# A rebuilt prologue for a transformer block on one core: two key halves, dummy products, four tiles normalised on GpSimd

## The chip, the cores and the metric

The kernel runs on one core of one Trainium2 chip. The metric is the device time of one execution in microseconds. The core has a tensor engine (PE, with its weight loads shown apart as PEld), VectorE (DVE), ScalarE (ACT), GpSimd (POOL) and SyncE (SP). SP issues nearly all DMAs here. Matrix products write into eight PSUM banks, from which DVE or ACT move results to the on-chip memory (SBUF).

## The reference, cut to what matters

One transformer block with 2048 tokens, width 1024, 32 heads of 32 columns which share one key head and one value head, and a gated feed-forward layer of 3584. All inputs are bf16. A conditioning row `c` gives six modulation vectors: shift, scale and gate for attention, and the same for the feed-forward layer.

```python
mod = (_silu(c) @ w_mod).reshape(c.shape[0], 6, 1, -1)
sa, ca, ga, sb, cb, gb = (mod[:, 0], ..., mod[:, 5])
h = _layernorm(x, axis=-1) * (1 + ca) + sa
q = (h @ wq) split into 32 heads; k = h @ wk; v = h @ wv      # one K and one V for all heads
p = softmax(q k^T * 32 ** -0.5, axis=-1)
x = x + ga * ((p v) merged @ wo)
h = _layernorm(x, axis=-1) * (1 + cb) + sb
x = x + gb * ((_silu(h @ w1) * (h @ w3)) @ w2)
```

## The kernel before, in words

**The planner.** `build` describes every instruction as a node of a graph (`G.add`) with its engine, what it reads and writes, a modelled duration and a priority (a lower number goes first). `Dag.schedule` is a list scheduler: it runs the graph on modelled engines and thereby fixes the order of instructions on each engine and the PSUM bank of each product group. `Dag.emit` then writes one instruction stream per engine with semaphore waits. So the order on every engine is fixed before the run, and an engine waits in that order. Products of scores (class S), of probabilities with V (class V) and of denominators (class D) go ahead of others on PE. A look-ahead for DVE stands at lines 205 to 216, but is switched off by `LOOK = 0.0` (line 13).

**The prologue (lines 454 to 825).** Tokens come as 16 tiles of 128 in `X`, which has 8 slots (`NXS`). For each tile `ln` computes LayerNorm statistics (on DVE by L509 and L511, for the tiles in `ONACT` on ACT by L519 and L523), a factor `RS` on POOL (L530, L532) and the normalised tile on DVE (L544). `tr` transposes four tiles at a time on PE (L558) into PSUM and evicts them into `HT` on ACT (L569) or DVE (L572). The modulation is not applied to the tokens: the scale `1 + ca` is multiplied into the rows of wq, wk, wv (L719, L721, L750), and the shift becomes a bias of each projection (L693 to L713, L741). Both come from the product L677 of `silu(c)` with eight slabs of w_mod, 512 KB each. `ORDER` (line 644) is the order of the loads behind the first eight X tiles:

```python
ORDER = ("w0", "w1", "w2", "w3", "x8", "x9", "w4", "x10", "x11", "w5", "w6", "w7", "q", "x12", "x13", "x14", "x15")
```

"w" is a slab of w_mod, "x" a token tile, "q" the first 128 columns of wq; the other 896 columns and wo follow. K (L608, evicted by L612) is made for 256, 256, 512, 512 and 512 tokens, V (L619, L622) four times for 512 tokens, Q (L629, L632) for 8 groups of four heads (f = 0 to 7), for the first 512 tokens in two parts. `gate` (L782, L787) makes two further modulation vectors, L794 multiplies wo by one of them, and L809 and L817 make the other two. The Q projections of the later tokens come last.

**Attention (lines 830 to 959).** It runs over 8 blocks of 256 query tokens. In a block, for each f, eight steps of 256 keys: scores (L855, eight small products into four of six PSUM banks), two exponentials on ACT (L865, 128x1024 elements each) into one of `NU = 11` buffers `U`, and tree adds of four steps' buffers into one of four `TR` buffers on DVE (L879, L884), with a fold of the two trees (L889) for f below 7. At the end of an f come its products with V (L902), and the denominator products of the f before with a selection matrix `SEL` (L922). L929 copies the numerators into `ASB`. When a group of f's is complete, L946 takes reciprocals, L952 spreads them over partitions and L957 multiplies; `RP` sets the priority of these for a block's last group (one value each for the first, the middle and the last blocks).

**After attention (`post`).** The output projection (L996, L1000), LayerNorm again, for the first and last block transposition on PE with eviction (L558, L581 or L575), then gate and up products (L1030), tanh (L1039) and multiplications on DVE (L1037, L1042, L1047), then the down product (L1064, L1070, L1076). `BP` sets the DVE priority of the part up to the transposition, again by block. Their weights come in a ring of six buffers (`RING`), which take over memory of the prologue: the first three need all Q projections done. `post` of a block overlaps attention of the next; only the last one stands alone.

Of the kernel before, what the change touches and what calls it, by code (L numbers as in the profile page):

```python
# [12 lines left out]
LOOK = 0.0  # L13
# [15 lines left out]
class Dag:  # L29


    def __init__(self, nc):
        self.nc = nc
        self.nodes = []
        self.last_write = {}
        self.readers = {}
        self.seq = 0
        self.dma_sems = {}
        self.last_acq = {}
        self.chain = 0  # L40

# [64 lines left out]
    def schedule(self, banks):  # L106
# [41 lines left out]
        while left:  # L148
# [56 lines left out]
            if e == "dve" and LOOK and n.dur > 0.9 and n.prio > 1:  # L205
                fin = None
                for b in banks:
                    g = bank_group[b]
                    rem = [x for x in g.nodes if x.start is None and x.eng == "pe"] if g is not None else []
                    if rem:  # L210
                        f1 = t_free["pe"] + sum(x.dur for x in rem) + 0.26
                        if fin is None or f1 < fin:
                            fin = f1
                if fin is not None and t < fin < t + LOOK:
                    t_free["dve"] = fin
                    continue
            ready[e].remove(n)
# [132 lines left out]
def build(nc, x_in, wq_in, wk_in, wv_in, wo_in, w1_in, w3_in, w2_in, c_in, wmod_in, out, S, D, F):  # L350
# [34 lines left out]
    BP = (0, 0, 0)  # L385
    WP = (4, 4, 4)
    RP = (0, 0, 0)
# [6 lines left out]
    RB = sb("RB", [P, QB], F32)  # L394
    WKR = sb("WKR", [P, NC, 4, 32], BF16)
    ASB = XN[:, 2:4, :].rearrange("p a d -> p (a d)").bitcast(F32).rearrange("p (a q) -> p a q", a=4)
    DSB = WKR[:].rearrange("p c a f -> p (c a f)").bitcast(F32).rearrange("p (a q) -> p a q", a=2)
# [25 lines left out]
    NR = len(RING)  # L423
    assert NF * QB + 2 * 4096 <= NC * S and NXS == 8
# [5 lines left out]
    WQ0R = WKR[:].rearrange("p c a f -> p c (a f)")  # L430
    WQ0K = ["WKR"]
# [20 lines left out]

    cuts = {}
    G.add("pool", lambda e: e.memset(SEL[:], 0.0), writes=["SEL"], dur=0.3)
    for a, fs in enumerate(DGRP):
        edge = [32 * j // len(fs) for j in range(len(fs) + 1)]
        for j, f in enumerate(fs):
# [4 lines left out]
    G.add("pool", lambda e: e.memset(IDENT[:], 0.0), writes=["IDENT"], dur=0.2)  # L462
    G.add("pool", lambda e: e.affine_select(IDENT[:], IDENT[:], pattern=[[-1, P]], compare_op=ALU.not_equal,
                                            fill=1.0, base=0, channel_multiplier=1),
          reads=["IDENT"], writes=["IDENT"], dur=0.4)

# [5 lines left out]
    def xload(t0, n):  # L472
        r = []
        for t in range(t0, t0 + n):
            r.append(dma(lambda e, t=t: e.dma_start(X[:, t % NXS, :], x2[t * P:(t + 1) * P, :]),
                         ("x", t % NXS), writes=[("X", t % NXS)], nbytes=P * D * 2))
        return r

    WQK = [("WREG", "q")]
    xload(0, 8)  # L480

    def wmload(k, after=()):
        return dma(lambda e, k=k: e.dma_start(WM01[:, k, :], wmod_in[k * P:(k + 1) * P, 0:2 * D]), ("wm01", k),
            writes=[("UR", k)], nbytes=P * 2 * D * 2, after=after)
# [50 lines left out]
    def xnt(q):  # L535

        return XN[:, q, :] if q < 4 else UREG[:, (NU + NTR - 2) * 2048 + (q - 4) * D:][:, 0:D]

    def xnk(q):
        return [] if q < 4 else [("UR", NU + NTR - 2 + (q - 4) // 2)]  # L540

    def ln_norm(t, q, s=None, bp=0):
        s = t % NXS if s is None else s
        G.add("dve", lambda e: e.tensor_scalar(xnt(q), X[:, s, :], MV[:, t, 0:1], RS[:, t:t + 1],  # L544
                                               ALU.subtract, ALU.mult),
              reads=[("X", s), ("RS", t), ("MV", t)], writes=[("XN", q)] + xnk(q), dur=0.42, prio=2 - bp)

    def ln_transpose(nt, q0, dst, dkeys, fs, fm, engs, prio=5, cbs=None, allow=None, bp=0):
# [3 lines left out]
        for cb in range(NC // ncb) if cbs is None else cbs:  # L552
            g = grp(allow)
            for i in range(nt):
# [6 lines left out]
                G.add("pe", tr, reads=[("XN", q0 + i), "IDENT"] + xnk(q0 + i), dur=ncb * 0.065, lat=0.2,  # L561
# [41 lines left out]
    def kproj(t0, n, allow=None):  # L603
        sl = slice(t0, t0 + n)

        def kmm(e, b, c):
            for gg in range(4):
                r = e.matmul(b[32 * gg:32 * gg + 32, 0:n], WKV[:, 0, c, :], HT[:, c, sl], start=c == 0, stop=c == NC - 1,  # L608
                             tile_position=(0, 32 * gg), skip_group_check=True)
            return r  # L610
        g = mm_group(NC, kmm, lambda c: WKK + hk(c, t0, n), n_cols=n, allow=allow, mode="V")
# [533 lines left out]
```

## Time and profile before

| | us |
|---|---|
| median of 4 runs (lowest to highest) | 1167.51 (1167.43 to 1167.62) |
| the profiled execution | 1167.55 |
| its span in the profile | 1165.7 |

| engine | busy us | share of the span |
|---|---|---|
| PE | 1114.3 | 96% |
| DVE | 1012.9 | 87% |
| ACT | 1028.4 | 88% |
| POOL | 43.0 | 4% |

The profile is of one execution. Times in it count from the start of its span. "Busy" of PE comes from modelled ends of pipelined products, so that a busy PE may still wait a little between them. In groups of instructions, a row names the line, the engine, the operation, the output and the inputs, how often it ran, and what ended the idle time before it (in square brackets after "<-"). The granted clock is that of the tensor engine, 1.00 being full speed. Attention's exponentials are 975.3 us of ACT's busy time; the first starts at 35.66 us and the last ends at about 1055.5.

### The profile page before, as it was taken

Reading aid. Unit: us, or ns where it says so; the run is one execution under the profiler, and the core shown is the slowest. Engines: PE = TensorE matmul, PEld = TensorE weight load, DVE = VectorE, ACT = ScalarE, POOL = GpSimd, SP = SyncE. Lnnn points to the kernel's source line nnn. Section 1 sums busy time; section 2 is a strip of 40 time slices with the busy share of each in tenths; the row PEclk is TensorE's granted clock in tenths of the full one; section 3 lists DMA queues with packets and bytes.
Section 4 is the critical chain, followed back from the end, with each engine's and each line's share of the span. In section 5 each row is a group of like instructions: output and inputs, shape, how many; then the busy total and the mean of one; then the engine's idle time right before and its main releaser. Section 6 shows DMA issues by size and latency. Waiting matters only on the chain.

```text
span 1165.7 us, 34946 instructions
## 1 busy us (share of the span) xinstructions
PE 1114.3 (96%) x15532; PEld 755.7 (65%) x15561; DVE 1012.9 (87%) x1504; ACT 1028.4 (88%) x1174; POOL 43.0 (4%) x86
## 2 busy tenths in 40 slices
PE   4998996999989999999999999999999999999998
PEld 4554442666657675767576766767567757677887
DVE  7778988898999999899989998999989998997452
ACT  3798999999999999999999999999999999992110
POOL 5100000000010001000000001000100000000000
PEclk9798998899999999999999999999999999999999
DMA  9616007455757565966596566856596659656995
GB/s 346 220 29 199 12 1 182 128 163 166 198 145 222 155 184 134 265 173 188 143 255 193 162 186 176 241 160 181 145 255 174 190 138 255 196 158 182 297 292 152
DMA packets 383222, 211.05 MB, mean 181 GB/s; under 512 B 21600, under 2 KB 374880, under 8 KB 383072
## 3 DMA queue, kind: packets, MB, share of 16 engines
q1 hardware_dynamic: 380992, 208.69, 63.7%
q8 instruction: 122, 2.00, 0.7%
q10 hardware_dynamic: 2080, 0.13, 0.1%
q14 instruction: 28, 0.23, 0.1%
HBM read 201.46 MB, written 4.19 MB: 176 GB/s over the span
## 4 chain that ended last, share of the span: by engine, by line
PE 74%; ACT 15%; DVE 8%; issue 2%; POOL 1%; DMA 0%; SPq 0%
PE PB L1030 24%; PE PB L1064 15%; ACT UREG L865 13%; PE SP L855 11%; PE PB L902 8%; PE PB L629 4%; PE PB L996 3%; PE SP L1030 3%; DVE UREG L884 2%; PE SP L1064 2%; DVE UREG L879 1%; PE PB L922 1%; PE PB L608 1%; DVE ST L509 1%; PE SP L558 1%
## 5 line engine op out<-in xcount | busy, mean ns | idle before, releaser
L865 ACT ACTIVATE UREG<-SP 128x1024 bf16<-128x1024 f32 x1024 | 975.3, 1121 | 17.2 <-PE SP L855 15.0
L884 DVE TENSOR_TENSOR UREG<-UREG 128x2048 bf16<-128x2048 bf16 x256 | 311.4, 1216 | 11.9 <-ACT UREG L865 9.6
L855 PE MATMUL SP<-QT,KT 32*128 32x256 bf16 x4096 | 206.1, 276 | 15.7 <-ACT UREG L865 14.4
L1030 PE MATMUL PB<-QT,WREG 128*128 128x256 bf16 x1632 | 205.4, 273 | 0.8 <-DVE WKR L940 0.4
L1030 PEld LDWEIGHTS PB<-QT,WREG 128*128 128x128 bf16 x1632 | 148.1, 98 | 46.8 <-issue 31.5
L879 DVE TENSOR_TENSOR UREG<-UREG 128x2048 bf16<-128x2048 bf16 x128 | 156.0, 1219 | 13.2 <-ACT UREG L865 9.7
L855 PEld LDWEIGHTS SP<-QT,KT 32*128 32x128 bf16 x4096 | 60.9, 92 | 139.0 <-ACT UREG L865 93.8
L1030 PE MATMUL PB<-QT,HREG 128*128 128x256 bf16 x1056 | 132.9, 273 | 0.6 <-DVE WKR L940 0.4
L902 PE MATMUL PB<-UREG,V 128*32 128x256 bf16 x4032 | 130.8, 277 | 1.4 <-ACT UREG L865 1.4
L902 PEld LDWEIGHTS PB<-UREG,V 128*32 128x32 bf16 x4032 | 99.9, 98 | 26.6 <-issue 17.1
L1030 PEld LDWEIGHTS PB<-QT,HREG 128*128 128x128 bf16 x1056 | 96.1, 98 | 29.6 <-issue 19.6
L1064 PE MATMUL PB<-WREG,HREG 128*128 128x256 bf16 x840 | 104.9, 273 | 0.5 <-DVE HREG L1042 0.5
L1064 PEld LDWEIGHTS PB<-WREG,HREG 128*128 128x128 bf16 x840 | 77.8, 98 | 22.2 <-issue 12.6
L1030 PE MATMUL PB<-QT,X 128*128 128x256 bf16 x544 | 69.1, 273 | 1.1 <-DVE WREG L1037 0.7
L889 DVE TENSOR_TENSOR UREG<-UREG 128x2048 bf16<-128x2048 bf16 x56 | 68.1, 1217 | 0.4
L629 PE MATMUL PB<-HREG,WREG 128*128 128x512 bf16 (+1 forms) x301 | 63.7, 349 | 4.0 <-DVE QT L632 1.6
L1064 PE MATMUL PB<-HREG 128*128 128x256 bf16 x532 | 67.1, 273 | 0.0
L1039 ACT ACTIVATE GSB<-GSB 128x512 bf16<-128x512 bf16 x56 | 42.3, 756 | 28.1 <-DVE GSB L1037 28.1
L1039 ACT ACTIVATE WREG<-WREG 128x512 bf16<-128x512 bf16 x56 | 43.4, 776 | 20.1 <-DVE WREG L1037 20.1
L1030 PEld LDWEIGHTS PB<-QT,X 128*128 128x128 bf16 x544 | 49.8, 98 | 15.8 <-issue 10.7
L1064 PEld LDWEIGHTS PB<-HREG 128*128 128x128 bf16 x532 | 49.2, 98 | 13.7 <-issue 7.8
L929 DVE COPY XN<-PB 128x256 f32<-128x256 f32 x63 | 26.5, 420 | 36.0 <-PE PB L922 34.1
(130 smaller groups left out, 1005.1 us busy)
## 6 DMA issues: line engine op xcount, KB each, us to landing
WREG<-in_B_w_dram SPq DMA_DIRECT2D x112, 512.0 KB, 5.1
HREG<-in_B_w_dram SPq DMA_DIRECT2D x74, 512.0 KB, 5.3
WREG<-in_B_w_dram SPq DMA_DIRECT2D x33, 896.0 KB, 5.0
X<-in_B_w_dram SPq DMA_DIRECT2D x38, 512.0 KB, 5.0
HREG<-in_B_w_dram SPq DMA_DIRECT2D x21, 896.0 KB, 5.3
X<-in_B_w_dram SPq DMA_DIRECT2D x10, 896.0 KB, 5.0
X<-in_A_x_dram SPq DMA_DIRECT2D x32, 256.0 KB, 5.4
WREG<-in_w_mod_dram SPq DMA_DIRECT2D x16, 512.0 KB, 5.3
```

The source lines that it names most:

```text
L629: g = mm_group(NC, lambda e, b, c: e.matmul(b[:, 0:n], WQ[:, c, f * P:(f + 1) * P], HT[:, c, sl], start=c == 0, stop=c == NC - 1), lambda ...
L855: r = e.matmul(SP[:, b, o:o + qn], KT[32 * gg:32 * gg + 32, kts[j] * P:(kts[j] + 1) * P], QT[32 * gg:32 * gg + 32, f, q0:q0 + qn], start=T ...
L865: G.add("act", lambda e, u=u, h0=h0, n=n, b0=b0, nb=nb: e.activation(U[:, u, h0 * W:(h0 + n) * W].rearrange("p (b w) -> p b w", b=nb), SP[ ...
L879: G.add("dve", lambda e, tr=tr, u=u, fu=first_u: e.tensor_tensor(TR[:, tr, 0:4 * W], U[:, fu, 0:4 * W], U[:, u, 0:4 * W], ALU.add), reads= ...
L884: G.add("dve", lambda e, tr=tr, u=u: e.tensor_tensor(TR[:, tr, 0:4 * W], TR[:, tr, 0:4 * W], U[:, u, 0:4 * W], ALU.add), reads=[("TR", tr) ...
L889: G.add("dve", lambda e, ta=ta, tb=tb: e.tensor_tensor(TR[:, ta, 0:4 * W], TR[:, ta, 0:4 * W], TR[:, tb, 0:4 * W], ALU.add), reads=[("TR", ...
L902: r = e.matmul(PB[g.bank][32 * gg:32 * gg + 32, 0:qn], V[:, kt, :], U[:, pu, (gg * npk + j) * qn:(gg * npk + j + 1) * qn], start=w0 + n == ...
L929: G.add("dve", lambda e, g=g, f=f: e.tensor_copy(ASB[:, f % 4, 0:qn], PB[g.bank][:, 0:qn]), writes=[("ASB", f % 4), ("XN", 2 + f % 4 // 2) ...
L996: g = mm_group(NC, lambda e, b, f, t=t, h=h: e.matmul(b, QT[:, f, t * P:(t + 1) * P], WO[:, f, h * 512:(h + 1) * 512], start=f == 0, stop= ...
L1030: return e.matmul(b[:, j * qn:(j + 1) * qn], w13[:, w, c, j * P:(j + 1) * P], QT[:, c, q0:q0 + qn], start=c == 0, stop=c == NC - 1)
L1039: G.add("act", lambda e, b=b: e.activation(TB[b], GS[b], ACT.Tanh, scale=0.5), reads=[("GS", b)], writes=[("TB", b)], clear=alias("TB") if ...
L1064: G.add("pe", lambda e, g=g, j=j, fc=fc, hf=hf, first=first, w2s=w2s: e.matmul(PB[g.bank][:, j * 256:(j + 1) * 256], HHT[:, hf * NH + fc, ...
```

## The change

Seven things are done at once.

1. **Loads.** The slabs of w_mod are cut into a half with the scale ("a") and a half with the shift ("s"). All 16 X tiles, the halves and three parts of wq (128, 384 and 512 columns) are in one `ORDER`. wq is loaded into the memory of wo (`WO`) and scaled from there into `WQ`; wo itself is loaded after the last of these reads. The scaled wk and wv have a memory of their own (`WKS`).
2. **Scale before shift.** The product with w_mod is in two groups, scale first; scaling of wk and of the first part of wq needs the scale alone. The biases come in three parts (`bias`).
3. **Normalised tiles** have 16 places instead of 8 (`xnt`, in memory not yet used). Tiles 9, 11, 13 and 15 are normalised on POOL. Statistics on ACT are now those of tiles 2 and 5. Tiles 0 to 7 are evicted by ACT, 8 to 15 by DVE. The first transposition of a group of four tiles waits for all four.
4. **Key halves.** In the first block f = 0 to 3 run over the first four steps of keys one after another, then over the other four; then f = 4 to 7 as before. For these eight pieces there are no tree adds: the denominator products read `U` directly, four buffers a piece. Numerators and denominators of the second piece are added to those of the first.
5. **Dummy products.** While the modelled time is below 250 us, the planner fills gaps on PE with 128-column products of the identity matrix into a bank that is free.
6. **Look-ahead for DVE** with new rules, for the whole kernel: before an operation of over 0.9 us (modelled; in the steady blocks the tree adds and folds) DVE waits up to 0.5 us for one of top priority, or up to 0.6 us for a product group in bank 0 or 1, if neither bank is free within 0.5 us.
7. **Priorities.** `BP` and `RP` are 5 for the first block, which puts the end of its attention and its second LayerNorm ahead of the tree adds on DVE. There the spreading of reciprocals has a buffer for each f, so that all are spread and then all multiplied.

```diff
-LOOK = 0.0
+LOOK = 0.5
+LK = 0.6
+LF = 0.5
+UP = -1
...
-            if e == "dve" and LOOK and n.dur > 0.9 and n.prio > 1:
...
+            if e == "dve" and n.dur > 0.9 and n.prio > UP:
+                soon = [c for c in cands if c[1].prio <= UP and c[0] < t + LOOK]
+                if soon:
+                    t_free[e] = min(c[0] for c in soon)
+                    continue
+                fin = t + LK
+                for b in (0, 1):
+                    i = bank_idle(b)
+                    if i is not None and i <= t + LF:
+                        fin = None
+                        break
                     g = bank_group[b]
...
+                        fin = min(fin, t_free["pe"] + sum(x.dur for x in rem) + 0.26)
+                if fin is not None and t < fin < t + LK:
+                    t_free[e] = fin
                     continue
+            if e == "pe" and self.warm is not None and t < self.warm[0]:
+                gap = s - t_free[e] - 0.3 - (0.1 if mode != "F" else 0.0) - (0.1 if n.mode != "F" else 0.0)
+                fb = [x for x in free_banks() if x[0] + SEM_LAT <= t_free[e]]
+                k = int(gap / self.warm[1])
+                if k > 0 and fb and self.warm[3].start is not None and self.warm[3].vis + SEM_LAT < t_free[e]:
...
+                    w.fn = self.warm[2](b, k)
+                    w.deps = [self.warm[3]]
+                    if bank_group[b] is not None:
+                        w.deps += [x for x in bank_group[b].nodes if x.eng != "pe"]
...
-    BP = (0, 0, 0)
+    BP = (5, 0, 0)
     WP = (4, 4, 4)
-    RP = (0, 0, 0)
+    RP = (5, 0, 0)
+    RBQ = (0,)
...
+    WARM = 250.0
+    HEAD = 4
+    DIRECT = (0, 1)
...
-    def ln_norm(t, q, s=None, bp=0):
+    def ln_norm(t, q, s=None, bp=0, en="dve"):
...
-        G.add("dve", lambda e: e.tensor_scalar(xnt(q), X[:, s, :], MV[:, t, 0:1], RS[:, t:t + 1],
+        G.add(en, lambda e: e.tensor_scalar(xnt(q), X[:, s, :], MV[:, t, 0:1], RS[:, t:t + 1],
...
-    ONACT = (3, 6)
...
+    ONACT = (2, 5)
+    ONPOOL = (9, 11, 13, 15)
+    KP = 1
+    QACT = 1
+    TRP = 1
+    EV = (("act",), ("act",), ("dve",), ("dve",))
+    ORDER = ("x0", "x1", "x2", "x3", "x4", "x5", "a0", "a1", "x6", "a2", "a3", "x7", "a4", "a5", "a6", "a7", "q0",
+             "s0", "s1", "s2", "s3", "s4", "s5", "s6", "s7", "q1", "x8", "x9", "x10", "x11", "x12", "x13", "x14", "x15", "q2")
+    QCUT = (0, 1, HEAD, NC)
...
+    def qscale(k):
+        a, b = QCUT[k] * P, QCUT[k + 1] * P
...
+        for c in range(NC):
+            wr = [("WQ", f, c) for f in ((HEAD,) if k == 2 else range(1, HEAD))]
+            if k == 1 and c % 2 < QACT:
+                G.add("act", lambda e, c=c: e.activation(WQ[:, c, a:b], WO[:, c, a:b], ACT.Identity, scale=MODC[:, 1, c:c + 1]),
...
+    bias(0, (0,), kb=True)
+    G.chain = 0
+    kproj(0, 256, (2, 3, 4, 5, 6, 7))
+    qproj(0, 256, 0, (2, 3, 4, 5, 6, 7), prio=1)
+    kproj(256, 256, (2, 3, 4, 5, 6, 7))
+    kproj(512, 512, (1,))
+    wscale(1, WVK)
+    qscale(1)
+    bias(1, (0,), vb=True)
+    qproj(0, 256, 1, (0, 1))
+    vproj(0, (0, 1))
+    vproj(1, (0, 1))
...
+        def step(f, s):
+            pend, trs = pends[f], trees[f]
+            direct = q0 == 0 and f < HEAD and s // per_t in DIRECT
...
+            pend.append((u, kts))
+            if direct:
+                return
...
+            if direct:
+                ds.append((f, pend, h))
+                dprev[0] = None
...
+                            a = U[:, a[0]] if us else TR[:, a]
...
+        if q0 == 0:
+            head = []
+            for h in range(2):
+                for f in range(HEAD):
+                    head += [(f, s) for s in range(h * per_t, (h + 1) * per_t)] + [(f, (h,))]
+            sched = head + [x for x in sched if x[0] >= HEAD]
...
+    def warm(b, k):
+        def f(e):
+            for _ in range(k):
+                r = e.matmul(PB[b][:, 0:P], IDENT[:], IDENT[:], start=True, stop=True, skip_group_check=True)
+            return r
+        return f
+    G.warm = (WARM, P / 2400.0 + 0.0026, warm, ident)
```

## The prediction

> **What bounds the kernel now.** I read the busy line by stage first, then the chain of waits that ended last, then the order of time of the first 62 us. Each row of the stage view below gives a stretch, its length, the busy time of PE, PEld, DVE, ACT and POOL, the granted TensorE clock (1.00 is full) and the DMA's share and rate.
>
> ```profile
> 0.00:35.66 35.66, 19.97 (x361) 16.68 (x365) 28.79 (x71) 14.62 (x27) 16.14 (x48) 0.90 0.99 353
> 35.66:60.00 24.34, 21.73 (x394) 13.19 (x390) 16.95 (x33) 20.12 (x26) 2.20 (x6) 0.79 0.51 162
> 60.00:170.00 110.00, 102.12 (x1378) 50.02 (x1390) 94.29 (x127) 105.71 (x113) 0.00 (x0) 0.95 0.20 64
> 170.00:211.00 41.00, 29.13 (x439) 13.55 (x440) 33.66 (x57) 36.63 (x39) 2.49 (x4) 0.79 0.52 129
> 211.00:383.00 172.00, 166.03 (x2416) 112.66 (x2411) 158.38 (x223) 171.31 (x196) 3.43 (x4) 1.00 0.63 176
> 383.00:1053.00 670.00, 667.09 (x9532) 455.90 (x9543) 625.18 (x902) 666.71 (x758) 17.15 (x20) 1.00 0.68 188
> 1053.00:1165.70 112.70, 108.26 (x1032) 93.70 (x1031) 55.62 (x98) 13.26 (x21) 1.58 (x4) 1.00 0.89 230
> ```
>
> From 383 us on PE and ACT are both full (667.1 and 666.7 of 670). The chain of waits runs on ACT's exponentials from about 223 to 383 and stays on PE afterwards, one step of it being:
>
> ```profile
> 543.75 0.33 PE SP L855 x8
> 544.08 1.96 PE PB L1030 x17
> ```
>
> So two engines are matched. A second saved early reaches the end only if both gain it: ACT has 1024 exponentials to run, PE has its products. PE's loss is all early: idle 15.7 us to 35.66, then 2.6, 7.9 and 11.9 us to 211, and 6.0 us to 383. A slow clock costs more: (1 - clock) times busy is 2.0 + 4.6 + 5.1 + 6.1 us. That is 44 + 18 = 62 us in all. ACT's early loss: no exponential before 35.66, 4.2 us idle to 60, 4.3 to 170, 4.4 to 211. The lines that show why:
>
> ```profile
> 24.29 0.55 PE L677 MATMUL PB<-SCT,UREG 128*128 128x1 bf16 x16
> 35.66 9.52 ACT L865 ACTIVATE UREG<-SP 128x1024 bf16<-128x1024 f32 x10 [0.47 <-PE SP L855]
> 45.01 2.37 ACT L569 ACTIVATE HREG<-PB 128x512 bf16<-128x512 bf16 x4
> 49.33 1.89 PE L629 MATMUL PB<-HREG,WREG 128*128 128x256 bf16 x8 [0.86 <-ACT HREG L569]
> 55.22 15.69 ACT L865 ACTIVATE UREG<-SP 128x1024 bf16<-128x1024 f32 x17 [4.05 <-PE SP L855]
> 175.94 7.21 SPq L1023 DMA_DIRECT2D WREG<-in_B_w_dram  x6
> 205.81 2.63 DVE L581 TENSOR_SCALAR QT<-PB,MODC 128x256 bf16<-128x256 bf16 x8
> 211.14 1.59 PE L1030 MATMUL PB<-QT,WREG 128*128 128x256 bf16 x13
> ```
>
> The modulation product waits for its last weights until 24.3; K, Q and the first exponential follow it. From 45 to 55 ACT evicts tiles 12 to 15 and then starves. From 176, when the last Q projection lets the gate/up weights load, to 211 PE has only attention and the output projection.
>
> **What the Trainium skill says.** "TensorE: Matmul & The Clock Gate", Part 1: the array is clocked at half rate after an idle window of about 3.4 us, full rate after as much sustained activity. The trace agrees: at 49.33 eight 256-column products took 1.89 us (0.236 each) at a granted 0.63, where 17 take 1.96 (0.115) at 1.00. "GPSIMD Engine Reference", Specifications: GpSimd shares its SBUF interfaces with VectorE, contention coming with two-input or two-port instructions. The trace agrees: a one-element RS op at 202.40 took 1.13 us under a tree add, 0.22 elsewhere. Section 3.1 there gives 1.8 cycles an element for a tight loop. "DMA: Bandwidth & Descriptors" puts the ceiling at 435 GB/s; here the first 20 us reach 390 to 420.
>
> **The change, part by part.**
>
> (a) Loads. Before the scale half of the modulation is complete there now lie 8 X tiles and 8 half slabs of 256 KB, 4.2 MB, then the first Q slice, then 2.1 MB of shift halves: 6.6 MB with K and V weights. Before it was 7.3 MB, with both halves finishing at 24.3. In 2-us slices the load curve of before has moved 4.35 MB by 14 us and 6.75 by 20, and a load lands 1 to 1.5 us after its bytes (w4, 5.4 MB in order, was consumed at 17.56). So scale at 15, shift at 21. SP issues 25 loads at 0.45 us from 0.72, all by 13 us: no bound.
>
> (b) First exponential. DVE normalises six of tiles 0 to 7 by about 18.5 (six times 1.28 + 0.2 of statistics, eight times 0.54, from 4.3). ACT then evicts all 16 banks' halves, 0.52 each, the last four tiles' by 23. Shift at 21.3, products 0.3, SAB copy 0.16, bias products 0.8, copy 0.15, K and Q evictions 0.47 + 0.48 at 24, S 0.4: first exponential at about 25 instead of 35.66, 10.7 earlier. The KT of keys 512 to 1023 is needed two steps (3.7 us) later and is there at 26 to 27.
>
> (c) Key halves. The head (f 0 to 3, keys 0 to 1023) is 32 exponentials, 29 us at 0.917, so ACT needs the keys of tiles 8 to 15 only at 54. They land by 29 (9.6 MB). Their DVE work is 8 x 1.48 of statistics, 4 x 0.54, 16 evictions x 0.41: 20 us, done by about 47. So the hole from 45 to 55 goes, 4.2 us idle and 4.3 of evictions (8 x 0.54), against about 1.7 for four Q scalings on ACT (4 x 384 elements, at the evictions' rate). ACT +6.7.
>
> (d) GpSimd. Four normalisations leave DVE, 4 x 0.54 = 2.2 us in a stretch where DVE is not last: worth nothing by itself. A GpSimd one isn't in the trace. From below: POOL's 128x512 copy took 0.61, so 1.2 for 1024. By the skill's 1.8 cycles at its 1.2 GHz: an estimate of 1.5. From above: 1.5 plus one 1.2-us hold under a two-input DVE op, 2.7. I take 1.5. Queued behind on POOL are the RS ops of the next tiles; two of them late by 1.5 still end before 54. With 2.7 it is 11 us of POOL and the 7-us cover is about used up. Price if gone: 0 to 4 us.
>
> (e) Denominators of the head by PE from U directly: per f 64 small products instead of 8 or 16. By L922's 8 in 0.22 us that is 1.77 against 0.22, times 4: PE +6.2, and splitting V's groups about +1 in switches. It takes 28 tree operations of 1.22 from DVE (34 us), adds 8 x 0.41.
>
> (f) Dummy products in PE's planned gaps, until the planner's 250 us. They replace idle time, so cost nothing where plan and chip agree; they also keep the clock up. At best they return most of the 18 us of slow clock, at worst (at half rate 0.107 for 0.056 each by the clock-gate page, in gaps the chip doesn't have) they delay PE by a few us. I take 14 us returned.
>
> (g) Priorities of block 0's ending. Reciprocals, shuffles and LayerNorm go ahead of the tree adds. From the last denominator product (173.6) to the first gate/up product (211.1) passed 37 us; the pure work is about 20 (copies 0.8, two reciprocals 1.9, two shuffles and multiplies 1.7, output projection 8 between attention steps, LayerNorm 4, evictions 2.6). As the Q projections would now end near 160 and attention of block 0 near 147, the two meet, and only the 7 us of weight load remain with little to do. PE idle there 5 instead of 11.9; ACT idle 4.4 down to 1.4.
>
> (h) DVE's look-ahead holds a tree add up to 0.6 us for a finishing PE group, in every block. In a steady block DVE is busy 117.4 of 126 us, so 8.6 us are free; 56 tree adds and folds can each wait 0.15 us before it bounds. Zero to 0.1 us each is hidden; above that see rival D.
>
> Sum, PE: idle 44 to about 29 (11 in the first 25 us, 3 to 60, 4 more to the boundary, 5, 6), so -15; slow clock -14; (e) +7: -22. ACT: 10.7 + 6.7 + 2 (half of the 4.3) + 3 = -22.4. They agree by chance of the balance; PE may also gain up to 8 us over ACT, since 12 us of the previous block's down projection fill its wait at the end. For a static order made from modelled durations I take off 2: -20 against the profiled execution's 1167.55 (span 1165.7 and 1.85 around it), which is the median to 0.04. Predicted 1147.
>
> **Rivals.** A, the sum: 1147, own range 1139 to 1155. Chance 0.58.
> B, only the start survives: PE stays saturated with Q projections until about 172 and the head's 7 us eat the clock gain; -10.7 and little else, 1157 (1155 to 1163). For it: PE is 93% busy from 60 to 170. Against: the holes after 170 are then still filled. 0.17.
> C, all early loss but the first 11 us is recovered: 62 - 11 - 7 - 12 (what ACT cannot give) = 32, 1135 (1129 to 1139). For it: the boundary's 37 us. Against: weights still load after the last Q projection. 0.12.
> D, slower: the look-ahead makes DVE the bound in steady blocks. 8.6 us a block are free; at a mean wait of 0.21 us for 56 operations DVE needs 129.2, 3.2 us a block more than 126, and over seven blocks that eats the 20 and more; at 0.25 us it is 5.4 x 7 - 20 = 18 us slower, 1185. For it: DVE is the third engine near full. Against: evictions of PE's groups seldom make it wait now (0.5 us a block before L1042). 0.10.
> E, no change: gains given back at the last block's tail, within 0.2% (2.3 us, about what a measurement of this kernel can tell from no change). 0.03.
>
> **Numbers.** 1147 is the likeliest case. The range, 1133 to 1160, takes in A, most of B and half of C. Faster 0.87, same 0.03, slower 0.10.
>
> **What would show it.** First exponential near 25 us (b); no ACT idle over 2 us before 60 (c); POOL tensor_scalar of 1024 elements at 1.2 to 2.7 us (d); granted clock 0.95 or more in each stretch to 211 (f); first gate/up product near 175 (g); 126 us a block after 383 (h). A first exponential after 30, a block over 127, or PE waiting at dummy products while attention is ready would make the prediction wrong.

## The result, and the profile after

| | before | changed |
|---|---|---|
| median of all runs beside each other | 1168.75 us (58 runs) | 1166.64 us (37 runs) |
| ratio, 95% interval | | 0.9977 (0.9970 to 0.9983) |
| span of the profiled execution | 1165.7 us | 1165.7 us |

The change saves 0.23%, 2.7 us of 1168.75, where 20 were forecast and the range ended 7 us below the time before. The profiled executions happen to have equal spans (the one before lies 1.2 us below its kernel's median, the changed one 0.9 above), so their stages can be laid side by side.

The stage view of the changed kernel, in the columns of the prediction (a stretch, its length, then the busy time of PE, PEld, DVE, ACT and POOL with the number of instructions, the granted clock, the DMA share and GB/s):

```profile
0.00:25.00 25.00, 18.02 (x314) 16.68 (x315) 14.44 (x33) 13.08 (x24) 11.37 (x38) 0.87 0.98 327
25.00:60.00 35.00, 24.74 (x488) 16.04 (x486) 24.21 (x63) 22.87 (x28) 21.53 (x20) 0.79 0.36 119
60.00:170.00 110.00, 103.53 (x1617) 55.24 (x1625) 71.94 (x114) 101.11 (x107) 0.00 (x0) 0.96 0.32 102
170.00:211.00 41.00, 38.51 (x537) 19.90 (x540) 39.84 (x68) 40.30 (x44) 3.31 (x4) 1.00 0.29 72
211.00:383.00 172.00, 163.42 (x2377) 110.07 (x2378) 155.55 (x219) 170.66 (x194) 3.48 (x4) 0.97 0.69 190
383.00:1053.00 670.00, 666.51 (x9532) 456.20 (x9541) 623.32 (x903) 667.44 (x758) 17.15 (x20) 1.00 0.68 188
```

Three things are to be seen. From 383 on the busy times of each engine agree within 2 us: nothing that the change gains is lost in the steady blocks. The boundary from 170 to 211 is nearly full now (PE 38.51 of 41, of it 0.90 dummies; before 29.13). And the stretch from 25 to 60, which was to be the full one, has PE idle for 10.3 us and the clock at 0.79.

What happens there stands in the view in order of time; these rows answer to the prediction's rows of before (what an instruction waited for is in brackets):

```profile
24.71 0.40 PE L713 MATMUL PB<-SCT,UREG 128*128 128x1 bf16 x8
29.16 3.83 ACT L925 ACTIVATE UREG<-SP 128x1024 bf16<-128x1024 f32 x4 [0.69 <-PE SP L915]
43.16 3.80 POOL L573 TENSOR_SCALAR WREG<-X,MV,RS 128x1024 bf16<-128x1024 bf16 x1
43.19 1.43 DVE L573 TENSOR_SCALAR WREG<-X,MV,RS 128x1024 bf16<-128x1024 bf16 x1
47.67 3.80 POOL L573 TENSOR_SCALAR WREG<-X,MV,RS 128x1024 bf16<-128x1024 bf16 x1
51.00 0.40 PE L915 MATMUL SP<-QT,KT 32*128 32x256 bf16 x8 [0.66 <-ACT UREG L925]
52.02 0.55 DVE L573 TENSOR_SCALAR GSB<-X,MV,RS 128x1024 bf16<-128x1024 bf16 x1 [2.36 <-POOL RS L553]
53.10 3.80 POOL L573 TENSOR_SCALAR GBB<-X,MV,RS 128x1024 bf16<-128x1024 bf16 x1
53.81 0.62 DVE L744 TENSOR_SCALAR WREG<-WO,MODC 128x512 bf16<-128x512 bf16 x1
57.05 0.59 PE L587 MATMUL PB<-IDENT,WREG 128*128 128x128 bf16 x4 [5.65 <-POOL GBB L573]
59.51 1.94 ACT L925 ACTIVATE UREG<-SP 128x1024 bf16<-128x1024 f32 x2 [5.82 <-PE SP L915]
59.62 0.34 DVE L744 TENSOR_SCALAR WREG<-WO,MODC 128x512 bf16<-128x512 bf16 x1
...
199.81 7.48 SPq L1134 DMA_DIRECT2D WREG<-in_B_w_dram  x6
202.31 2.64 DVE L610 TENSOR_SCALAR QT<-PB,MODC 128x256 bf16<-128x256 bf16 x8
206.25 1.26 PE L1141 MATMUL PB<-QT,WREG 128*128 128x256 bf16 x10
```

A normalisation on GpSimd takes 3.80 us. The four form a chain from 35.5 to 56.9, with the small `RS` operations and a wait for DVE's statistics between them. The first transposition of tiles 12 to 15 waits for all four tiles (the change made its reads so), PE works in its fixed order, and the score step behind it waits with it: PE stands 5.65 us and ScalarE 5.82. (ScalarE's wait is not GpSimd's alone, as e1 will show.) The gate/up weights are still issued late, at 199.81 (before 175.94), and the first gate/up product starts at 206.25 (before 211.14).

The chain of waits in the steady part is what it was, PE's scores and products in turn:

```profile
543.83 0.33 PE SP L915 x8
544.16 1.96 PE PB L1141 x17
```

How many of the 1024 exponentials have started by a given time shows where a lead is won and lost (counted from one trace each; an exponential is 0.917 us):

| by (us) | 50 | 60 | 70 | 100 | 170 | 211 | 383 |
|---|---|---|---|---|---|---|---|
| before | 11 | 18 | 29 | 60 | 130 | 168 | 344 |
| changed | 17 | 21 | 28 | 58 | 127 | 169 | 343 |
| changed, normalised on DVE (e1) | 17 | 24 | 32 | 64 | 136 | 177 | 350 |
| the same without dummies (e5) | 20 | 24 | 35 | 66 | 138 | 179 | 352 |
| the same kernel again (e14) | 18 | 24 | 34 | 65 | 133 | 172 | 346 |

The changed kernel leads by six at 50 us and by none at 70. Two profiles of the same kernel (e5, e14) differ by one at 70 us, but by six at 383: differences of that size in the late columns are not a part's doing.

### The profile page after: what moved, and what is told of

Same layout as the page of the kernel before. It is cut to its first block, busy times and chain, and to the rows that moved or that the text cites. A ratio compares the mean times of both kernels' runs of the same rounds, so it can differ in the third digit from the quotient of the medians.

```text
span 1165.7 us, 35655 instructions
## 1 busy us (share of the span) xinstructions
PE 1123.0 (96%) x15880; PEld 767.8 (66%) x15908; DVE 984.6 (84%) x1494; ACT 1028.7 (88%) x1170; POOL 58.5 (5%) x90
## 4 chain that ended last, share of the span: by engine, by line
PE 91%; DVE 3%; ACT 2%; POOL 1%; DMA 1%; issue 1%; SPq 1%; DVEq 0%
PE PB L1141 33%; PE PB L1175 16%; PE SP L915 14%; PE PB L975 10%; PE PB L658 4%; PE PB L1107 4%; PE SP L1141 3%; PE SP L1175 2%; PE PB L1002 2%; ACT UREG L925 2%; DMA UREG<-in_w_mod_dram 1%; DVE ST L530 1%; PE PB L637 1%; PE PB L838 0%; DMA WREG<-in_w_mod_dram 0%
## 5 line engine op out<-in xcount | busy, mean ns | idle before, releaser
L948 DVE TENSOR_TENSOR UREG<-UREG 128x2048 bf16<-128x2048 bf16 x240 | 291.9, 1216 | 12.5 <-ACT UREG L925 10.1
L915 PE MATMUL SP<-QT,KT 32*128 32x256 bf16 x4096 | 205.8, 275 | 12.2 <-ACT UREG L925 11.8
L942 DVE TENSOR_TENSOR UREG<-UREG 128x2048 bf16<-128x2048 bf16 x120 | 146.0, 1217 | 11.8 <-ACT UREG L925 6.0
L1175 PE MATMUL PB<-WREG,HREG 128*128 128x256 bf16 x812 | 101.2, 273 | 0.0
L1175 PEld LDWEIGHTS PB<-WREG,HREG 128*128 128x128 bf16 x812 | 75.3, 98 | 20.4 <-issue 11.4
L551 POOL TENSOR_SCALAR RS<-MV 128x1 f32<-128x1 f32 x32 | 19.3, 608 | 1008.4 <-DVE MV L532 1008.2
L957 DVE TENSOR_TENSOR UREG<-UREG 128x2048 bf16<-128x2048 bf16 x52 | 63.3, 1218 | 0.5
L1150 ACT ACTIVATE GSB<-GSB 128x512 bf16<-128x512 bf16 x56 | 38.7, 690 | 27.5 <-DVE GSB L1148 27.5
L1014 DVE COPY XN<-PB 128x256 f32<-128x256 f32 x63 | 26.5, 421 | 39.3 <-PE PB L1002 38.8
L1175 PEld LDWEIGHTS PB<-HREG 128*128 128x128 bf16 x532 | 49.2, 98 | 14.3 <-issue 8.0
L1141 PEld LDWEIGHTS PB<-QT,X 128*128 128x128 bf16 x528 | 48.2, 98 | 14.3 <-issue 9.3
```

The source lines that it names most:

```text
L915: r = e.matmul(SP[:, b, o:o + qn], KT[32 * gg:32 * gg + 32, kts[j] * P:(kts[j] + 1) * P], QT[32 * gg:32 * gg + 32, f, q0:q0 + qn], start=T ...
L942: G.add("dve", lambda e, tr=tr, u=u, fu=first_u: e.tensor_tensor(TR[:, tr, 0:4 * W], U[:, fu, 0:4 * W], U[:, u, 0:4 * W], ALU.add), reads= ...
L948: G.add("dve", lambda e, tr=tr, u=u: e.tensor_tensor(TR[:, tr, 0:4 * W], TR[:, tr, 0:4 * W], U[:, u, 0:4 * W], ALU.add), reads=[("TR", tr) ...
L957: G.add("dve", lambda e, ta=ta, tb=tb: e.tensor_tensor(TR[:, ta, 0:4 * W], TR[:, ta, 0:4 * W], TR[:, tb, 0:4 * W], ALU.add), reads=[("TR", ...
L1014: G.add("dve", lambda e, g=g, f=f: e.tensor_copy(ASB[:, f % 4, 0:qn], PB[g.bank][:, 0:qn]), writes=[("ASB", f % 4), ("XN", 2 + f % 4 // 2) ...
L1141: return e.matmul(b[:, j * qn:(j + 1) * qn], w13[:, w, c, j * P:(j + 1) * P], QT[:, c, q0:q0 + qn], start=c == 0, stop=c == NC - 1)
```

## The experiments

All times stand beside runs of the kernel before on the same chip; "us" of a difference is the difference of two ratios times 1168.75. Theory at the start: GpSimd's 3.80 us and what PE's order queues behind it take the gain. Rivals: the look-ahead (the prediction's D), the denominators by PE, and PE's work itself.

| | edit | ratio (95% interval) |
|---|---|---|
| e1 | changed, all normalised on DVE | 0.9932 (0.9920 to 0.9944) |
| e2 | changed, GpSimd planned at 3.8 us | 0.9962 (0.9949 to 0.9976) |
| e3 | before, four tiles on GpSimd | 1.0076 (1.0059 to 1.0094) |
| e4 | e1 without look-ahead | 1.0040 (1.0027 to 1.0054) |
| e5 | e1 without dummies | 0.9914 (0.9893 to 0.9935) |
| e14 | e5 again | 0.9925 (0.9904 to 0.9947) |
| e6 | e1 without denominators from U | 0.9959 (0.9944 to 0.9974) |
| e7 | before with the look-ahead | 0.9997 (0.9984 to 1.0011) |
| e8 | e1 without the priorities | 0.9961 (0.9945 to 0.9977) |
| e9 | e5, Q projections of the head first | 0.9939 (0.9922 to 0.9957) |
| e10 | e5 without key halves | 1.0037 (1.0022 to 1.0052) |
| e11 | e9 with GpSimd | 0.9946 (0.9928 to 0.9965) |
| e12 | e9, denominators from U in one half | 0.9957 (0.9941 to 0.9973) |
| e13 | changed without dummies | 0.9973 (0.9959 to 0.9986) |

Before plans are compared, one thing that all traces show. The 6th and the 7th block (128 exponentials each) take 126.1 us in the kernel before, in the changed one and, to 0.2 us, in every other run but e4. What follows the last exponential differs: 110.2 us in the kernel before, the changed one, e1, e3, e5, e6, e7, e10, e13 and e14; 114.1 in e2, e9, e11 and e12; 115.0 in e8; 126.7 in e4. The order of DVE's instructions in the 6th and 7th block goes with it: it is one and the same in the changed kernel, e1, e5, e6, e10, e13 and e14, and another, the same one, in e2, e8, e9, e11 and e12. So a small edit in the prologue can tip the plan into another order of the later blocks, which costs 4 to 5 us at the end. Comparisons within one group (e1, e5, e6, e10, e13 and e14 with each other and with the changed kernel; e3 with before; e11 and e12 with e9) are free of this; those across groups (e2, e8, e9 against e1 or e5) are not.

**GpSimd taken out (e1), planned at its true price (e2), and put into the old kernel (e3).**

```diff
-    ONPOOL = (9, 11, 13, 15)
+    ONPOOL = ()
```

> The changed kernel with all 16 tiles normalised on VectorE. Theory P (the four GpSimd normalisations, 3.80 us each instead of the 1.2 planned, hold PE in its fixed order until 57 us): the PE wait of 5.7 us before the last tile's transposition and ACT's waits of 5.8 and 2.1 us go, 10 to 14 us less, 1153 to 1157. Rival L (the late loads for the gate products and PE's load after 60 us take back any earlier gain): at most 3 us less, 1164 to 1167.

```diff
-dur=0.42 if en == "dve" else 1.2, prio=2 - bp)
+dur=0.42 if en == "dve" else 3.8, prio=2 - bp)
```

> The changed kernel with the same GpSimd normalisations, but the planner is told 3.8 us for each instead of 1.2, so only the order on the engines differs. Theory P, if the harm is PE's order (attention steps queued behind a transposition that waits): 4 to 9 us less than the changed kernel. If the harm is the GpSimd chain itself (keys of tiles 8 to 15 late whatever the order): within 3 us of the changed kernel. Rival L: no difference.

```diff
-        ln_norm(t, t % 8)
+        ln_norm(t, t % 8, en="pool" if t in (9, 11, 13, 15) else "dve")
```

(with `en` and the price of 1.2 us in `ln_norm`, as in the change)

> The kernel before with only one part of the change: tiles 9, 11, 13 and 15 normalised on GpSimd, planned at 1.2 us. Theory P: 4 x (3.8 - 0.54) = 13 us of longer chain, of which the transpositions of tiles 8 to 11 and 12 to 15 wait for most; 6 to 14 us slower than before, 1174 to 1182. Rival L: PE is the bound and the prologue's slack hides it, within 2 us of before.

Without GpSimd the changed kernel gains 5.3 us more (0.9977 to 0.9932), half of the 10 to 14 expected. PE's wait is gone, but ScalarE's is not:

```profile
62.43 13.47 ACT L925 ACTIVATE UREG<-SP 128x1024 bf16<-128x1024 f32 x14 [5.56 <-PE SP L915]
```

So PE's idle time is what GpSimd adds; ScalarE also waits here because PE has other work first.

e2 misses its 4 to 9 us: in time it isn't told apart from the changed kernel (0.9962 and 0.9977, the intervals overlapping), which is what was expected if the chain itself did the harm. Its trace says otherwise. With GpSimd's true duration in the plan PE has no wait for POOL between 30 and 70 us, ScalarE has 26 exponentials by 60 us (e1 24) and 351 by 383 (e1 350), and the last one ends at 1047.6 us (e1 1048.8, changed 1055.5). It is the end behind the last exponential, 114.1 us instead of 110.2, that puts e2 3.5 us behind e1. That PE's order does the harm rests on the trace, then, not on e2's time.

In the old kernel the same four tiles cost 8.9 us, as expected. There PE's waits are plain, in the rows of PE, ACT and POOL in order of time:

```profile
28.89 0.61 PE L558 MATMUL SP<-IDENT,XN 128*128 128x128 bf16 x4 [4.06 <-POOL XN L544]
34.74 0.82 PE L558 MATMUL SP<-IDENT,XN 128*128 128x128 bf16 x6 [3.45 <-POOL XN L544]
42.22 7.68 ACT L865 ACTIVATE UREG<-SP 128x1024 bf16<-128x1024 f32 x8 [0.68 <-PE SP L855]
```

Two waits of 4.06 and 3.45 us stand before the first scores (at most 1.31 there in the kernel before), and the first exponential comes at 42.22 instead of 35.66.

**The look-ahead (e4, e7): the prediction's rival D.**

```diff
-            if e == "dve" and n.dur > 0.9 and n.prio > UP:
+            if e == "dve" and LOOK and n.dur > 0.9 and n.prio > UP:
...
-LOOK = 0.5
+LOOK = 0.0
```

> As e1_norm_dve, and the look-ahead of VectorE switched off for the whole kernel. Theory P says nothing of it: within 2 us of e1. Rival D of the prediction (look-ahead holds VectorE in each of eight blocks): 3 us or more faster than e1, with a shorter steady block.

```diff
-            if e == "dve" and LOOK and n.dur > 0.9 and n.prio > 1:
+            if e == "dve" and n.dur > 0.9 and n.prio > UP:
```

(with the rest of the new look-ahead behind it, in the kernel before)

> The kernel before with the look-ahead of VectorE alone. If the look-ahead is what keeps PE fed in every block (e1 against e4: 13 us): 3 us or more faster than before. If the 13 us were a property of those two plans only, since PE of the kernel before is 99.6% busy from 383 us on: within 2 us of before.

D falls. Without the look-ahead e1 loses 12.6 us, which neither side had expected, and the old kernel is the same with it. The loss isn't in the prologue: e4 has 352 exponentials by 383, and e1 350. The stage row of e1:

```profile
383.00:1053.00 670.00, 667.57 (x9595) 457.29 (x9588) 622.81 (x907) 663.22 (x752) 17.15 (x20) 1.00 0.68 188
```

and of e4:

```profile
383.00:1053.00 670.00, 657.84 (x9498) 449.60 (x9497) 619.87 (x898) 659.58 (x748) 14.88 (x20) 1.00 0.67 183
```

PE is idle 2.4 us in the first and 12.2 in the second, with nothing in those blocks edited but the rule by which they are planned. The blocks are no longer for it (124.9 to 126.7 us each); the work that PE leaves undone comes due at the end. These are the last exponentials of e1 (span 1159.0) and of e4 (1171.3):

```profile
1045.69 3.09 ACT L925 ACTIVATE UREG<-SP 128x1024 bf16<-128x1024 f32 x3
...
1040.77 3.84 ACT L925 ACTIVATE UREG<-SP 128x1024 bf16<-128x1024 f32 x4
```

e4 finishes attention 4.2 us before e1, and then needs 126.7 us instead of 110.2. As the old kernel without the rule idles only 2.9 us from 383 to 1053, the rule isn't needed as such; 12.6 us is the look-ahead's worth in one plan.

**The denominators from U (e6) and the priorities (e8).**

```diff
-    DIRECT = (0, 1)
+    DIRECT = ()
```

> As e1_norm_dve, with key halves, but the denominators of the eight pieces from tree adds on VectorE again instead of from PE (64 products per f instead of 16). If PE's extra 6 us (term e) count: 2 to 6 us faster than e1. Rival: VectorE is late between 35 and 60 us and needs the relief: 3 us or more slower.

```diff
-    BP = (5, 0, 0)
+    BP = (0, 0, 0)
...
-    RP = (5, 0, 0)
+    RP = (0, 0, 0)
```

> As e1_norm_dve, with the priorities of block 0's ending as before (BP and RP 0). Term g says they bring the gate/up products forward: 3 to 7 us slower than e1, PE idle from 170 to 211 back near 10 us. Rival: the Q projections end too late for it to matter: within 2 us.

Without either, e1 is about 3 us slower (0.9959 and 0.9961 against 0.9932). For e6 the reason is in the head: with the tree adds back on DVE, the evictions of tiles 8 to 15 come later and ScalarE starves for 10.48 us:

```profile
59.24 11.22 ACT L925 ACTIVATE UREG<-SP 128x1024 bf16<-128x1024 f32 x12 [10.48 <-PE SP L915]
```

With the tree adds left on it, then, DVE is the late engine of that stretch.

For e8 the number came as expected, 3.4 us, but the reason isn't shown. PE's idle time from 170 to 211, dummies counted as idle, is 7.6 us (e1 4.8; near 10 was expected), the first gate/up product comes at 200.60 (e1 198.17), and yet the last exponential ends earlier than in e1 (1047.0, e1 1048.8). What follows it takes 115.0 us instead of 110.2. So e8 is another plan of the later blocks too, and what the priorities do by themselves isn't known.

**The dummy products (e5, e14, e13).**

```diff
-    G.warm = (WARM, P / 2400.0 + 0.0026, warm, ident)
+    G.warm = None
```

> As e1_norm_dve, without dummy products. If they return most of the slow clock, as the prediction says (term f, 14 us): 8 to 14 us slower than e1, granted clock below 0.9 from 60 to 260 us. Rival: the gaps that they fill are short and the clock of the first 60 us stays at half whatever they do, while they can hold real products up: within 3 us of e1, either sign.

> The earlier run without dummy products and with all normalisations on VectorE, the same kernel again on the same chip as the run before. Expected as then: 0.989 to 0.993 of the kernel before, 1157 to 1160; it is the fastest version if it stays below 0.9939, which the run with the Q projections first had.

> The changed kernel with only the dummy products taken out; the four normalisations stay on GpSimd and the Q projections where they were. Theory 'order': PE still stands idle some 5 us before the transposition of tile 15 with score steps behind it, so 4 to 7 us slower than the run beside it without GpSimd's normalisations, 1162 to 1165. Rival 'GpSimd only with dummies': within 2 us of it, 1157 to 1160.

The dummies return nothing: e5 and e14 against e1, and e13 against the changed kernel (0.9973 and 0.9977), are equal within their intervals. The stage view of L1216 alone (PE and PEld only) in the changed kernel says why:

```profile
0.00:25.00 25.00, 9.26 (x110) 7.87 (x110) 0.87 0.98 327
25.00:60.00 35.00, 0.00 (x0) 0.00 (x0) 0.79 0.36 119
60.00:170.00 110.00, 0.00 (x0) 0.00 (x0) 0.96 0.32 102
```

They fill gaps that the plan has, while it waits for loads. The gap of 5.65 us at 51 is one that the plan doesn't have. e13 also answers what GpSimd costs without them. It stands 5.6 us behind e14 on the same chip, in the same group of plans, with the same wait as in the changed kernel:

```profile
56.97 0.58 PE L587 MATMUL PB<-IDENT,WREG 128*128 128x128 bf16 x4 [5.66 <-POOL GBB L573]
59.43 4.00 ACT L925 ACTIVATE UREG<-SP 128x1024 bf16<-128x1024 f32 x4 [5.82 <-PE SP L915]
```

**The hole that is left (e9), and GpSimd in another order (e11).** Without GpSimd, e5 still starves before 60 us:

```profile
45.24 9.27 ACT L925 ACTIVATE UREG<-SP 128x1024 bf16<-128x1024 f32 x10 [1.12 <-PE SP L915]
57.89 1.05 PE L658 MATMUL PB<-HREG,WREG 128*128 128x256 bf16 x8
59.63 0.40 PE L915 MATMUL SP<-QT,KT 32*128 32x256 bf16 x8
60.08 3.89 ACT L925 ACTIVATE UREG<-SP 128x1024 bf16<-128x1024 f32 x4 [5.57 <-PE SP L915]
```

The step needs the Q of f 3, whose product stands behind the transpositions of tiles 8 to 15.

```diff
-    qproj(0, 256, 1, (0, 1))
+    qproj(0, 256, 1, (0, 1), prio=0)
...
-        qproj(0, 256, f, (0, 1))
+        qproj(0, 256, f, (0, 1), prio=0)
```

> The changed kernel with all normalisations on VectorE and no dummy products, and with the Q projections of f 1 to 3 at priority 0, ahead of the transpositions of tiles 8 to 15. In the run without dummies ScalarE starved for 5.57 us before 60.08 because the score step needed the Q of f 3, which stood behind those transpositions (Q product at 57.89). Theory 'early lead': the hole goes, ScalarE has 5 to 6 exponentials more at 70 us than that run's 35, and as one exponential is 0.92 us the end moves by as much: 1153 to 1155. Rival 'PE's total': PE was busy 5.0 of 5.0 us through the hole, so nothing is won for the engine that is full later; 1157 to 1160.

> As the run with the Q projections first, without dummies, but with the four normalisations on GpSimd and planned at 1.2 us as in the changed kernel. Theory: the GpSimd chain of four times 3.80 us (first start near 35.5, last end near 57) holds PE before the transposition of tile 9 and again of tile 13 whatever stands around it, and the score steps planned between them wait: 4 to 7 us slower than the Q-first run, 1158 to 1161. Rival: with Q ahead ScalarE has work of its own for the whole of the chain and GpSimd costs under 2 us, 1154 to 1156.

The hole goes and nothing is won: 28 exponentials by 60 us instead of 24, but 35 by 70 in both, because PE was busy in the hole with work that now comes after it. So "PE's total" is the better theory for the lead. The time says less: e9 (0.9939) isn't faster than e5 (0.9914 and 0.9925), but its end behind the last exponential is 3.9 us longer, which could hide a gain of that size. e11, of the same group as e9, was a miss in the other direction: GpSimd, forecast to cost 4 to 7 us, costs 0.8 here (0.9946 against 0.9939), not told from nothing, though up to some 4 us fit the intervals. PE still waits once for it, 2.60 us before 45.04; the wait before the last tile is gone. Its rows show the cover:

```profile
51.15 4.15 POOL L573 TENSOR_SCALAR GBB<-X,MV,RS 128x1024 bf16<-128x1024 bf16 x1
...
51.34 1.70 PE L637 MATMUL PB<-HREG,WKS 128*32 128x512 bf16 x28
53.52 1.05 PE L1002 MATMUL PB<-UREG,SEL 128*32 128x256 bf16 x32
56.10 0.28 PE L587 MATMUL PB<-IDENT,GSB 128*128 128x128 bf16 x2
...
56.10 7.44 ACT L925 ACTIVATE UREG<-SP 128x1024 bf16<-128x1024 f32 x8 [0.75 <-PE SP L915]
```

Score steps, products of the other tiles' keys and denominators lie between 50 and 55; the transpositions come when the chain has ended at 55.3.

**The key halves (e10).** The head taken f by f:

```diff
-            for h in range(2):
-                for f in range(HEAD):
+            for f in range(HEAD):
+                for h in range(2):
```

> The run without dummies (all normalisations on VectorE), with the head taken f by f, both key halves of one f before the next f, in place of one key half over all four f. Only 8 exponentials then stand ahead of the first that needs the keys of tiles 8 to 15. Theory 'early lead': ScalarE stops near 36 us until those keys exist at about 55, 8 to 14 exponentials at 60 us instead of 24, end 10 to 14 us later, 1169 to 1173. Rival 'PE's total': PE pulls the same products forward into the stop, no more than 4 us later, 1159 to 1163.

As the first theory had it: 8 exponentials from 40 to beyond 50 us, one wait of 15.09 us, and 1.0037 against the 0.9920 of e5 and e14 (their mean), 13.7 us. All are of one group of plans.

```profile
54.61 3.77 ACT L925 ACTIVATE UREG<-SP 128x1024 bf16<-128x1024 f32 x4 [15.09 <-PE SP L915]
```

**One half of the head's denominators back to the trees (e12).**

```diff
-    DIRECT = (0, 1)
+    DIRECT = (0,)
```

> As the run with the Q projections first, with the denominators taken by PE from U for the first key half of the head only (the second half goes back to VectorE's tree adds: 14 operations of about 1.22 us, 17 us, between 60 and 100 us where VectorE is 40 to 60 per cent busy; PE saves about 3 us). Theory 'PE's total': PE is the full engine after 383 us, so 1 to 3 us faster than the Q-first run. Rival: VectorE is needed for evictions there, as it was when both halves were taken from the trees (4.6 us slower); 1 to 3 us slower.

0.9957 against 0.9939, the intervals overlapping: not told apart.

The lowest ratios are those of e5, the change without GpSimd and without dummies: 1158.74 and 1161.48 us in its two sets, where the kernels before beside it had 1168.89 and 1168.79. One profile of it spans 1156.6 us and the other 1162.5, so differences of 2 or 3 us between e1, e5, e9, e11 and e12 aren't read as any part's doing, and e5 isn't shown to be faster than e1.

## Why the prediction was wrong

The step that failed most is (c) with (d): "So the hole from 45 to 55 goes ... ACT +6.7", resting on GpSimd normalisations of 1.5 us and a 7-us cover that would hide them. They took 3.80 us, and the price was 5.3 us. The second is (f): 14 us of clock from dummy products that return no time.

One reading of the view has to be set right first. Its clock column begins with the first entry of the clock's record and counts the time before as 1.00. That entry comes at 22.2 us in the profile before, at 8.3 in the changed one, at 30.5, 23.4 and 18.6 in e13, e5 and e14. Before it PE runs at half speed in all of them: 107 ns pass from one 128-column product to the next, as in the stretches recorded as 0.50. In those recorded as 1.00 it is 56 ns. So the 0.90 of the first stretch was too high, and the slow clock of before cost 22 us, not 18. (Also, the 0.63 beside the product at 49.33 is the mean from 40 to 50; during it the record has 0.50, which fits its 0.236 us better.)

The working counted PE's idle time as 44 us and took it to 29, and the slow clock as 18 and took it to 4. Measured over the same stretches (rounded), dummies counted as idle, and the slow clock as half of PE's busy time at half speed:

| | before | forecast | changed | e13 | e5 | e14 |
|---|---|---|---|---|---|---|
| PE idle, first 25 us | 13.1 | 11 | 14.3 | 12.5 | 12.8 | 12.9 |
| 25 to 60 | 5.2 | 3 | 10.3 | 9.6 | 5.9 | 5.0 |
| 60 to 170 | 7.9 | 4 | 6.5 | 4.0 | 6.1 | 3.9 |
| 170 to 211 | 11.9 | 5 | 3.3 | 2.7 | 4.2 | 4.7 |
| 211 to 383 | 6.0 | 6 | 8.6 | 8.1 | 8.6 | 8.4 |
| idle, sum | 44 | 29 | 43 | 37 | 38 | 35 |
| slow clock | 22 | 4 | 15 | 19 | 13 | 19 |
| both | 66 | 33 | 58 | 56 | 50 | 54 |

Off the gains go 7.7 us for the head's denominators on PE. That leaves 0.6 us for the changed kernel, 2.5 for e13, 8.1 for e5 and 4.3 for e14; the spans of their profiles are shorter than before's by 0.0, 1.9, 9.1 and 3.2. For these four the account closes to about 1 us; for e1, e3, e6 and e10 it is 3 to 5 us too kind, so it supports that PE's own time decides, but doesn't prove it. Of the forecast's 22 us the changed kernel misses 7 between 25 and 60, 7 in the clock, and about 3 or less in each other stretch.

- (a) held roughly: the scale slabs came in time for K, but the last shift product ended near 25 instead of 21. (b) First exponential at 29.16, not 25: PE takes the last shift products and the transpositions of tiles 4 to 7 in turn until 25.3, at half speed, and ACT's evictions of these tiles end at 26.5 instead of 23. The clock is not all of it, as e4 has full speed from 11.2 on and its first exponential at 29.05. 6.5 of 10.7 us came.
- (c) The mechanism was right and is the largest part of the change: e10 prices it at 13.7 us. The hole did not go, though: 5.82 us of ScalarE's wait remain (5.56 in e1, without GpSimd), and at 60 us it leads by 3 exponentials where 17.4 us of lead (10.7 + 6.7) were forecast.
- (d) The term that was mis-sized. 3.80 us is above the upper bound of 2.7. "GPSIMD Engine Reference", Section 3.1, gives 1.8 cycles an element as the best case, a tight loop; at its 1.2 GHz this operation, with two scalars from pointers, ran at 4.5 (3.80 us for 1024), and the measurement decides. Four of these and what lies between them are 21 us, not 6, and the cover of "about 7" was gone. The price measured, 5.3 us (e1) and 5.6 us (e13 against e14), exceeds even the bound of 4 given for the cover gone. It isn't GpSimd's time as such, but what PE's order, planned with 1.2 us, puts behind it: told the truth the plan has no such wait in its trace (e2), and in another order the cost can't be measured (e11). A stretch at half clock lies on the gap as well (52.6 to 62.8; e1 has 1.00 there), so how much of the 5.3 us is idle time and how much clock isn't separated.
- (e) PE pays for the denominators: they are 25.5 us of its time before and 33.2 now, 7.7 more, where about 7 were forecast. But the relief of DVE's trees, costed at nothing, is worth more: about 3 us for the pair (e6).
- (f) 14 us of clock were counted; 7 came in the changed kernel's profile, but in time the dummies return nothing. They do raise the clock early: full speed from 8.3 us, in e13 from 30.5. There PE has little to do, as it waits for loads. They all but end at 25 us, and the half clock from 39.0 to 45.8 and from 52.6 to 62.8 comes after them. Two profiles of one kernel differ by 6 us of slow clock (e5, e14), so smaller differences in that row say nothing.
- (g) Right in the hole (PE idle 3.3 instead of 11.9), wrong in the date: 206 instead of 175. Q projections filled the boundary, their last evictions being at 199.87, as rival B said ("PE stays saturated with Q projections"). What was deferred by the key halves is PE's work still: by 60 us the kernel before had made K for all 2048 keys, the changed one for 1024.
- (h) Hidden, as forecast; a middle block takes 126.1 us before and after. Rival D is refuted by e4 and e7.

Not settled: what in the prologue tips the planner into one or the other order of the later blocks, which is 110.2 or 114.1 us behind the last exponential, and what the priorities of (g) are worth by themselves.

## What to carry to other kernels

An operation that moves to another engine is priced by a row of the same form on that engine; if there is none, its price is an open term, and what counts is not its length but what stands behind its consumer in the fixed order there. Work that is hidden or deferred on the engine that is full later isn't won: count that engine's own work done by a given time, not only the lead of the engine it feeds. Fillers placed by a plan land in the gaps the plan knows, and the gaps that cost are those it doesn't. And before a small difference between two plans is put down to an edit, look whether the order of the parts that were not edited stayed the same.

## What was unexpected of the hardware

- GpSimd's two-operation tensor_scalar of 128x1024 bf16 took 3.80 us, DVE's 0.54. Side by side they disturbed each other only at the start. DVE operations of this kind (bf16, SBUF to SBUF) that began within 0.8 us after GpSimd's, with none of them running before, ended 1.33 to 1.47 us after its start, whatever their usual length: the normalisation at 43.19 took 1.43 instead of 0.54, L744 at 53.81 0.62 instead of the 0.34 at 59.62. Those that began more than 1.2 us into GpSimd's operation ran at their usual 0.34 and 0.54 (e2, e11), and statistics and copies out of PSUM beside it kept their times. Where such an operation or a tree add was running when GpSimd began, it was GpSimd that took longer: 4.02 (e2), 4.15 (e11), 4.34 and 4.58 (e3). "GPSIMD Engine Reference", Specifications, puts contention at DVE instructions in a two-port mode or with two inputs; which of these DVE's normalisation is, no run here shows. The pattern looks as if GpSimd kept DVE out for about the first microsecond of its 3.80; that is a reading of these traces.
- A clock of 1.00 in the view can be time without a record. These are rows of the changed kernel and of e5, without dummies, with the same work from 20 to 25:

```profile
20.00:25.00 5.00, 5.00 (x83) 4.54 (x84) 0.03 (x1) 2.82 (x6) 0.00 (x0) 0.50 1.07 357
23.90 1.01 PE L587 MATMUL SP<-IDENT,UREG 128*128 128x128 bf16 x8
...
20.00:25.00 5.00, 5.00 (x100) 4.33 (x93) 0.51 (x2) 2.87 (x6) 0.00 (x0) 1.00 1.07 358
21.72 1.01 PE L587 MATMUL SP<-IDENT,UREG 128*128 128x128 bf16 x8
23.72 0.61 PE L587 MATMUL SP<-IDENT,UREG 128*128 128x128 bf16 x8
```

  Eight products take 1.01 us in both; e5's become fast, 0.61, only behind its first entry at 23.4. Products of known size are the better clock.
- Dummies do release the clock, and don't keep it. "TensorE: Matmul & The Clock Gate", Part 1, releases the half rate after some 3.4 us of sustained activity. In the changed kernel the dummies begin at 5.2 us, run at half speed until 8.3 and at full speed to 18.5, which agrees. Then the clock falls, after 3.4 us with 1.70 of PE at work, and stays at half for 6.8 us with PE busy in all of them; in e1 it is 10.2 us, from 19.8, so here the release took two to three times as long. Of the six profiles with dummies five fall to half clock between 18 and 21 us; e4 doesn't.
